# Splitting the last queries' scores of a block-causal attention into 256 and 320 columns instead of 512 and 64

## The chip, the cores and the metric

The kernel runs on one NeuronCore of a Trainium2 chip. Its engines are TensorE (PE; its weight loads are shown apart, as PEld), VectorE (DVE), ScalarE (ACT), GpSimd (POOL) and SyncE (SP, which here only issues DMAs). The metric is the device time of one execution in microseconds, lower is better. One execution was also profiled, instruction by instruction.

## What is computed

The reference is a block-causal attention, then two feed-forward layers, all in float32:

```python
# q, k, v: (4, 8, 576, 64): batch, heads, positions, head size
scores = q @ k.transpose(0, 1, 3, 2) / sqrt(64)
scores = where(pos[:, None] // 64 >= pos[None, :] // 64, scores, -1e9)
attn = exp(scores - scores.max(-1)); attn = attn / (attn.sum(-1) + 1e-9)
x = (attn @ v) as (2304, 512)
h = x @ w_in;  x = (h * sigmoid(h)) @ w_out               # w_in (512, 2048), w_out (2048, 512)
h = x @ w_in2; out = (max(h, 0) + alpha * min(h, 0)) @ w_out2
```

The last 64 of the 576 positions form the last block; their queries see all 576 keys, so no mask is needed for them.

## The kernel before

Attention goes in jobs of one batch and two heads. There are 8 `FirstJob`s and 8 jobs of kind 0 for the first 256 positions of the batches, then 16 jobs of kind 1, each for positions 256 to 575 of two heads. Beside them PE runs the first feed-forward layer: `up1` (tiles `h`) and `down1` (tiles `acc`) come in pairs of 24 products of 256 columns, all recorded at L786. The second layer follows after about 530 us with products of 384 and 512 columns, also at L786.

A product of two float32 operands is made of three matmuls (high by high, high by low, low by high part), each of which loads its own 128-column weights.

In a job of kind 1, PE has five groups beside L786. The text calls them by letters:

- B: `scores(2)`, two heads side by side, six matmuls of 384 columns at L539, into one PSUM tile `e` and the PSUM tile `s`
- C: `scores(3)`, six matmuls of 512 columns at L539, into two tiles `e`; a small product at L517 (`bound`) stands behind it
- A: `last_scores`, the 64 last queries of both heads (128 rows) against 576 keys at L539: three matmuls of 512 columns into `s`, then three of 64 columns into a tile `e`. This is what the change touches
- O: `output` at L660 (24 float16 matmuls), which in the program stands just ahead of A of the same job
- the last output at L730 (28 short matmuls), two jobs behind A

PSUM has one buffer `s` and two buffers `e`, used in turn: A of one job and B of the next share `s`. B therefore starts on `s` only when ACT has read A's scores from it.

Behind A come, on DVE, the largest score of each part (L681 and L683) and the smaller of the two negated maxima (L685); on ACT (L301) the exponentials with their sums; on DVE the sums and the reciprocal (L698, L700, L702); on POOL and DVE the weights in two float16 parts (L712, L714); then a DMA transposes them. Near A, DVE also makes the low parts `qk` of a later job's queries and keys (L504, L507), after ACT made the high parts; ACT begins that job's `qk` tile when A, the last reader of the tile's old contents, is done. L639 and L637 are weights of `scores` on DVE and POOL; L819 and L311 belong to the first layer's activation; L753 takes an output out of PSUM.

The order of everything is written by a planner at build time. Each operation is added with a cost from a formula and a due time; `Plan.order` runs through these and fixes one order for each engine. So an edit to the costs or to what waits for what can move instructions on all engines. The cost of a PE group is

```python
def pe_cost(*columns, gap=13.0):
    return sum(max(n, 56) / 2.4 + gap for n in columns) * 1e-3
```

Of the kernel before, what the change touches and what calls it, by code (L numbers as in the profile page):

```python
# [13 lines left out]
AF = mybir.ActivationFunctionType  # L14
ALU = mybir.AluOpType
AX = mybir.AxisListType
# [4 lines left out]
EPS = 1e-9  # L21
P_EXP = 14
# [187 lines left out]
def dve_cost(n, per_cycle=1, pointers=0):  # L210
    return (68 + 60 * pointers + n / 0.96 / per_cycle) * 1e-3
# [10 lines left out]
def pe_cost(*columns, gap=13.0):  # L222
    return sum(max(n, 56) / 2.4 + gap for n in columns) * 1e-3
# [3 lines left out]
def block_causal_attention_silu_prelu(  # L227
# [13 lines left out]
    nc = tc.nc  # L241
# [14 lines left out]
    add = plan.add  # L256
# [6 lines left out]
    psum = ctx.enter_context(tc.tile_pool(name="psum", bufs=1, space=PSUM))  # L263
# [31 lines left out]
    def act(n, dst, src, func, reads, writes, psum=False, **kw):  # L295
        pointers = sum(callable(kw.get(x)) for x in ("scale", "bias"))
        cost = act_cost(n, psum, pointers, "accum_out" in kw)

        def fn():
            k = {x: y() if callable(y) else y for x, y in kw.items()}  # L300
            nc.scalar.activation(dst(), src(), func, **k)  # L301

        return add("ACT", cost, fn, reads, writes)
# [162 lines left out]
    class Job:  # L466
# [203 lines left out]
        def last_scores(self):  # L670

            qk = self.qk
            x = sb(att_p, [128, 10], F32, "stat", 4, name="stat4")
            s, s2 = ps_scores(self.k), ps_scores(self.k)
            def products():
                for dst, a, b in ((s, 0, 512), (s2, 512, 576)):
                    for f in self.product(dst()[:, 0:b - a], slice(0, 128), 256, 128, a, b):
                        f()

            add("PE", pe_cost(*[512] * 3, *[100] * 3), products, [qk], [s, s2], after=self.beside(-1, "output"))  # L680
            add("DVE", dve_cost(512), lambda: nc.vector.tensor_reduce(  # L681
                x()[:, 0:1], s(), axis=AX.X, op=ALU.max, negate=True), [s], [(x, 0)])
            add("DVE", dve_cost(64), lambda: nc.vector.tensor_reduce(  # L683
                x()[:, 1:2], s2()[:, 0:64], axis=AX.X, op=ALU.max, negate=True), [s2], [(x, 0)])
            add("DVE", dve_cost(80), lambda: nc.vector.tensor_tensor(  # L685
                x()[:, 2:3], x()[:, 0:1], x()[:, 1:2], op=ALU.min), [(x, 0)], [(x, 1)])
            p = sb(att_p, [128, 512], F32, "p", 3)
            pb = sb(att_p, [128, 64], F32, "p4b", 2)
            bias = lambda: x()[:, 2:3]
            act(512, lambda: p(), lambda: s(), AF.Exp, [s, (x, 1)], [p, (x, 2)], psum=True,  # L690
                bias=bias, accum_out=lambda: x()[:, 4:5])
            act(64, lambda: pb(), lambda: s2()[:, 0:64], AF.Exp, [s2, (x, 1)], [pb, (x, 3)], psum=True,
                bias=bias, accum_out=lambda: x()[:, 5:6])
            self.xp[4] = x, p, pb

        def last_weights(self):
            x, p, pb = self.xp.pop(4)
            add("DVE", dve_cost(1, 1, 1), lambda: nc.vector.tensor_scalar(  # L698
                x()[:, 6:7], x()[:, 4:5], x()[:, 5:6], EPS, op0=ALU.add, op1=ALU.add), [(x, 2), (x, 3)], [(x, 4)])
            add("DVE", dve_cost(1), lambda: nc.vector.tensor_scalar(  # L700
                x()[:, 6:7], x()[:, 6:7], 2.0**-P_EXP, None, op0=ALU.mult), [(x, 4)], [(x, 4)])
            add("DVE", dve_cost(6), lambda: nc.vector.reciprocal(x()[:, 8:9], x()[:, 6:7]), [(x, 4)], [(x, 5)])  # L702
            rr = lambda: x()[:, 8:9]
            p16 = self.parts16(0)
            hl = lambda: p16()[:, 0:8].rearrange("p (j c) m -> p j c m", c=2)
            p3 = lambda: p().rearrange("p (j m) -> p j m", m=128)
            for src, n, hi, lo, key in (
                (p3, 512, lambda: hl()[:, :, 0], lambda: hl()[:, :, 1], 0),
                (lambda: pb(), 64, lambda: p16()[:, 8, 0:64], lambda: p16()[:, 8, 64:128], 2),
            ):  # L710
                b = pb if key else p
                add("POOL", pool_cost(n), lambda src=src, hi=hi: nc.gpsimd.tensor_scalar(  # L712
                    hi(), src(), rr(), 1.0, op0=ALU.mult, op1=ALU.mult), [b, (x, 5)], [(p16, key)])
                add("DVE", dve_cost(n, 1, 1), lambda src=src, hi=hi, lo=lo: nc.vector.scalar_tensor_tensor(  # L714
                    lo(), src(), rr(), hi(), op0=ALU.mult, op1=ALU.subtract),
                    [b, (x, 5), (p16, key)], [(p16, key + 1)])
            pT = self.pT4 = sb(att_p, [128, 9, 128], F16, "pT4")
            self.transpose(lambda: pT(), lambda: p16().rearrange("p a m -> p (a m)"), 9, [p16], [pT])

# [251 lines left out]
    for d in range(-20, total + 1):  # L971
        attend(d + 1.0)
        n, c = seq[d] if 0 <= d < total else (NB, 0)
# [37 lines left out]
    for s in range(N2 * MF + 1):  # L1011
        n, m = divmod(s, MF)
# [102 lines left out]
```

## Time and profile before

| | |
|---|---|
| Time, median of 3 runs | 977.61 us (976.92 to 980.19) |
| The profiled execution's own time | 975.61 us |
| Its span, first to last instruction | 973.8 us |
| PE busy | 956.1 us (98%) |
| DVE, ACT, POOL busy | 597.0, 398.5, 213.8 us |
| Mean granted TensorE clock | 0.998 |

The profiled execution took 1.8 us more than its span, and 2.0 us less than the median of the runs. Busy shares are averages over stages. The jobs of kind 1 lie between about 188 and 460 us; their 16 groups A start between 202 and 454 us, 16.8 us apart.

### The profile page before, as it was taken

The numbers are of one execution on the slowest core, as the hardware profiler recorded it, in microseconds if no ns is written. First come the engines' busy times: TensorE is split into PE (matmuls) and PEld (weight loads), VectorE is DVE, ScalarE is ACT, GpSimd is POOL, SyncE is SP. The second block draws the span as 40 slices with busy tenths as digits, with TensorE's granted clock in tenths as the row PEclk, the third lists the DMA queues.
The fourth block names the chain that finished last, engine by engine and source line by source line (L and its number), as shares of the span: only waits on it lengthen the run. The fifth ranks groups of instructions, "written<-read, shape, count | busy, mean of one in ns | idle before, by whom it ended". The sixth has DMA issues, their size and how long they took to land.

```text
span 973.8 us, 17935 instructions
## 1 busy us (share of the span) xinstructions
PE 956.1 (98%) x7008; PEld 882.4 (91%) x7008; DVE 597.0 (61%) x1343; ACT 398.5 (41%) x928; POOL 213.8 (22%) x262
## 2 busy tenths in 40 slices
PE   7799999999999999999999999999999999999998
PEld 4699999999999999999999999999999999999997
DVE  4899966578877778776113899544443444434443
ACT  7997645455555555553234656211211211211111
POOL 0002313344545445453234200100100100100000
PEclk9999999999999999999999999999999999999999
DMA  9941243356565656564116950010100200000100
GB/s 366 346 198 49 59 115 87 101 111 120 136 143 127 125 129 138 109 133 79 33 55 225 368 209 1 1 66 1 33 33 0 65 1 1 33 1 1 33 1 33
DMA packets 124468, 94.04 MB, mean 97 GB/s; under 512 B 98400, under 2 KB 109792, under 8 KB 124384
## 3 DMA queue, kind: packets, MB, share of 16 engines
q1 hardware_dynamic: 124384, 92.90, 34.4%
q8 instruction: 55, 0.90, 0.4%
q14 instruction: 29, 0.24, 0.1%
HBM read 60.37 MB, written 9.96 MB: 72 GB/s over the span
## 4 chain that ended last, share of the span: by engine, by line
PE 89%; DMA 5%; DVE 3%; ACT 1%; issue 1%; POOL 0%; SPq 0%; POOLq 0%; DVEq 0%; ACTq 0%
PE h L786 29%; PE acc L786 27%; PE e L786 16%; PE s L786 7%; DMA raw0i<-w_in 4%; PE e L539 3%; PE o L660 2%; PE s L539 2%; PE o L730 1%; PE o L517 1%; DMA pT<-p 1%; DVE p L639 1%; DMA raw1i<-w_in 0%; ACT p L301 0%; POOL p L637 0%
## 5 line engine op out<-in xcount | busy, mean ns | idle before, releaser
L786 PE MATMUL h<-xh,w0i 128*128 128x256 f32 x1728 | 229.2, 287 | 1.0 <-DVE w0i L344 0.6
L786 PEld LDWEIGHTS h<-xh,w0i 128*128 128x128 f32 x1728 | 215.8, 193 | 3.5 <-DVE w0i L344 1.0
L786 PE MATMUL acc<-g,w0o 128*128 128x256 f32 x1536 | 201.2, 285 | 0.1
L786 PEld LDWEIGHTS acc<-g,w0o 128*128 128x128 f32 x1536 | 189.7, 192 | 1.6 <-issue 0.5
L301 ACT ACTIVATE g<-u 128x384 fp32r<-128x384 f32 x96 | 50.2, 523 | 270.0 <-DVE u L904 270.0
L786 PE MATMUL e<-w1o,g 128*128 128x512 f32 x576 | 148.8, 394 | 0.0
L786 PEld LDWEIGHTS e<-w1o,g 128*128 128x128 f32 x576 | 106.8, 188 | 16.7
L786 PE MATMUL h<-xh,w1i 128*128 128x384 f32 x576 | 109.1, 337 | 0.0
L786 PE MATMUL acc<-xh,w1i 128*128 128x384 f32 x576 | 108.8, 337 | 0.0
L786 PEld LDWEIGHTS h<-xh,w1i 128*128 128x128 f32 x576 | 102.3, 188 | 4.1
L786 PEld LDWEIGHTS acc<-xh,w1i 128*128 128x128 f32 x576 | 102.4, 188 | 4.0
L311 POOL TENSOR_TENSOR g<-t,g 128x512 fp32r<-128x512 f32 x56 | 77.7, 1387 | 86.6 <-ACT g L301 84.4
L819 DVE SCALAR_TENSOR_TENSOR t<-t,h 128x512 f32<-128x512 f32 x72 | 49.1, 682 | 65.0 <-ACT t L301 64.8
L311 DVE TENSOR_TENSOR g<-u,g 128x384 fp32r<-128x384 f32 x96 | 54.5, 567 | 54.7 <-ACT g L301 54.7
L637 POOL TENSOR_SCALAR p<-p,stat 128x384 f16<-128x384 f32 (+3 forms) x96 | 61.9, 651 | 99.4 <-DVE stat L626 36.4
L786 PE MATMUL s<-w1o,g 128*128 128x512 f32 x288 | 82.0, 393 | 0.0
L311 POOL TENSOR_TENSOR xh<-xs,xh 128x384 fp32r<-128x384 f32 x24 | 25.0, 1071 | 255.0 <-ACT xh L301 255.0
L301 ACT ACTIVATE t<-h 128x512 f32<-128x512 f32 x72 | 43.2, 599 | 82.2 <-PE h L786 77.5
L639 DVE SCALAR_TENSOR_TENSOR p<-p,stat,p 128x384 f16<-128x384 f32 (+3 forms) x96 | 68.6, 730 | 10.4 <-POOL p L637 10.1
L902 DVE TENSOR_SCALAR u<-acc,alpha_sb 128x384 f32<-128x384 f32 x48 | 29.6, 618 | 73.4 <-PE acc L786 73.4
L902 DVE TENSOR_SCALAR u<-h,alpha_sb 128x384 f32<-128x384 f32 x48 | 29.7, 618 | 69.7 <-PE h L786 69.5
L786 PEld LDWEIGHTS s<-w1o,g 128*128 128x128 f32 x288 | 54.1, 188 | 12.5
(113 smaller groups left out, 1154.7 us busy)
## 6 DMA issues: line engine op xcount, KB each, us to landing
st<-qkv_b SPq DMA_DIRECT2D x16, 800.0 KB, 4.7
raw0i<-w_in SPq DMA_DIRECT2D x16, 512.0 KB, 10.2
raw0o<-w_out SPq DMA_DIRECT2D x16, 512.0 KB, 10.2
raw1i<-w_in SPq DMA_DIRECT2D x16, 512.0 KB, 5.7
raw1o<-w_out SPq DMA_DIRECT2D x16, 512.0 KB, 5.6
x<-x2e SPq DMA_DIRECT2D x18, 256.0 KB, 3.4
st<-qkv_first SPq DMA_DIRECT2D x8, 512.0 KB, 8.2
st<-qkv_a SPq DMA_DIRECT2D x8, 512.0 KB, 3.9
```

The lines of the kernel that those rows point to most:

```text
L301: nc.scalar.activation(dst(), src(), func, **k)
L311: eng.tensor_tensor(lo(), src(), hi().bitcast(F32), op=ALU.subtract)
L517: add("PE", 0.25, lambda: nc.tensor.matmul(t()[:, 0:128], am()[:, 0:1].to_broadcast([128, 128]), eye_sb(), start=True, stop=True), [am, ey ...
L539: yield lambda n=n, a=a, b=b: nc.tensor.matmul(dst, w[rows, a, q0:q0 + m], w[rows, b, nq + k0:nq + k1], start=(n == 0), stop=(n == 2))
L637: add("POOL", pool_cost(n), lambda hl=hl, rr=rr, pr=pr: nc.gpsimd.tensor_scalar(hl()[:, :, 0], pr(), rr(), 1.0, op0=ALU.mult, op1=ALU.mult ...
L639: add("DVE", dve_cost(n, 1, 1), lambda hl=hl, rr=rr, pr=pr: nc.vector.scalar_tensor_tensor(hl()[:, :, 1], pr(), rr(), hl()[:, :, 0], op0=A ...
L660: nc.tensor.matmul(o()[64 * r:64 * r + 64, q0:T1], self.v(r, kt, cv), self.pT[r][1]()[:, 2 * kt + cp, q0:T1], start=(kt == 0 and n == 0), ...
L730: nc.tensor.matmul(o()[64 * r:64 * r + 64, 0:64], self.v(r, kt, cv), pT()[:, run, 64 * r:64 * r + 64], start=(run == 0 and cv == 0), stop= ...
L786: nc.tensor.matmul(dst, lhs(a), rhs(b), start=(start and n == 0), stop=(stop and n == 2))
L819: add("DVE", dve_cost(2 * T1), lambda: nc.vector.scalar_tensor_tensor(t(), t(), 1.0, h3(), op0=ALU.add, op1=ALU.mult), [t, h], [t])
L902: add("DVE", dve_cost(T2, 1, 1), lambda: nc.vector.tensor_scalar(u(), h()[:, 0:T2], 0.0, alpha_sb()[:, m:m + 1], op0=ALU.min, op1=ALU.mult ...
```

## The change

The 576 keys are divided at 256 instead of at 512. A becomes three matmuls of 256 columns into `s` and three of 320 columns into `e`. The two reductions take 256 and 320 columns. The exponentials become three instead of two: 256 columns from `s`, 256 columns and 64 columns from `e`, so that the tiles `p` and `pb` hold the same as before. The three sums are added in one instruction; the small constant and the scale go into the next one.

```diff
             def products():
-                for dst, a, b in ((s, 0, 512), (s2, 512, 576)):
+                for dst, a, b in ((s, 0, 256), (s2, 256, 576)):
...
-            add("PE", pe_cost(*[512] * 3, *[100] * 3), products, [qk], [s, s2], after=self.beside(-1, "output"))
-            add("DVE", dve_cost(512), lambda: nc.vector.tensor_reduce(
-                x()[:, 0:1], s(), axis=AX.X, op=ALU.max, negate=True), [s], [(x, 0)])
-            add("DVE", dve_cost(64), lambda: nc.vector.tensor_reduce(
-                x()[:, 1:2], s2()[:, 0:64], axis=AX.X, op=ALU.max, negate=True), [s2], [(x, 0)])
+            add("PE", pe_cost(*[256] * 3, *[320] * 3), products, [qk], [s, s2], after=self.beside(-1, "output"))
+            add("DVE", dve_cost(256), lambda: nc.vector.tensor_reduce(
+                x()[:, 0:1], s()[:, 0:256], axis=AX.X, op=ALU.max, negate=True), [s], [(x, 0)])
+            add("DVE", dve_cost(320), lambda: nc.vector.tensor_reduce(
+                x()[:, 1:2], s2()[:, 0:320], axis=AX.X, op=ALU.max, negate=True), [s2], [(x, 0)])
...
-            act(512, lambda: p(), lambda: s(), AF.Exp, [s, (x, 1)], [p, (x, 2)], psum=True,
-                bias=bias, accum_out=lambda: x()[:, 4:5])
-            act(64, lambda: pb(), lambda: s2()[:, 0:64], AF.Exp, [s2, (x, 1)], [pb, (x, 3)], psum=True,
-                bias=bias, accum_out=lambda: x()[:, 5:6])
+            for dst, src, n, c in (
+                (lambda: p()[:, 0:256], lambda: s()[:, 0:256], 256, 4),
+                (lambda: p()[:, 256:512], lambda: s2()[:, 0:256], 256, 5),
+                (lambda: pb(), lambda: s2()[:, 256:320], 64, 6),
+            ):
+                part = (pb, (x, c)) if c == 6 else ((p, c), (x, c))
+                act(n, dst, src, AF.Exp, [s if c == 4 else s2, (x, 1)], part, psum=True,
+                    bias=bias, accum_out=lambda c=c: x()[:, c:c + 1])
...
-                x()[:, 6:7], x()[:, 4:5], x()[:, 5:6], EPS, op0=ALU.add, op1=ALU.add), [(x, 2), (x, 3)], [(x, 4)])
+                x()[:, 7:8], x()[:, 4:5], x()[:, 5:6], x()[:, 6:7], op0=ALU.add, op1=ALU.add),
+                [(x, 4), (x, 5), (x, 6)], [(x, 7)])
...
-                x()[:, 6:7], x()[:, 6:7], 2.0**-P_EXP, None, op0=ALU.mult), [(x, 4)], [(x, 4)])
-            add("DVE", dve_cost(6), lambda: nc.vector.reciprocal(x()[:, 8:9], x()[:, 6:7]), [(x, 4)], [(x, 5)])
+                x()[:, 7:8], x()[:, 7:8], EPS, 2.0**-P_EXP, op0=ALU.add, op1=ALU.mult), [(x, 7)], [(x, 7)])
+            add("DVE", dve_cost(6), lambda: nc.vector.reciprocal(x()[:, 8:9], x()[:, 7:8]), [(x, 7)], [(x, 8)])
```

The new lines move the later ones: L786 of before is L791 of the change, L730 is L735, L819 is L824, L753 is L758, and L698, L700 and L702 are L702, L705 and L707.

The planner answers with another order from the first group A on. PE, from A of the eighth job of kind 1 to B of the next job, before:

```order
L539 MATMUL s<-qk 128x512 x3
L539 MATMUL e<-qk 128x64 x3
L786 MATMUL acc<-g,w0o_914 128x256 x12
L786 MATMUL acc<-g,w0o_945 128x256 x12
L786 MATMUL h<-xh_3078,w0i_1154 128x256 x12
L539 MATMUL e<-qk 128x384
L539 MATMUL s<-qk 128x384
```

The same place on PE in the changed kernel:

```order
L539 MATMUL s<-qk 128x256 x3
L539 MATMUL e<-qk 128x320 x3
L791 MATMUL acc<-g,w0o_914 128x256 x12
L791 MATMUL acc<-g,w0o_945 128x256 x12
L539 MATMUL e<-qk 128x384
L539 MATMUL s<-qk 128x384
```

B moved ahead of 12 products of `up1`: it stands 24 instead of 36 products behind A. So it is in 10 of the 15 jobs that have a B behind their A; in the other five it is 42, 36, 30, 27 and 27 products. Before, it stood 36 products behind in 11 of the 15 jobs. C moved with it: in most jobs from 30 products ahead of the next O to 48, in three to 36.

DVE at the same place, from the activation L819 of the first layer to the sums behind A, before:

```order
L819 SCALAR_TENSOR_TENSOR t<-t,h 128x512
L639 SCALAR_TENSOR_TENSOR p_4713<-p,stat,p_4713 128x4x128
L639 SCALAR_TENSOR_TENSOR p_4716<-p,stat,p_4716 128x4x128
L753 SCALAR_TENSOR_TENSOR xh_4180<-o,sc,xh_4180 128x256
L681 TENSOR_REDUCE stat_4746<-s 128x1
L504 SCALAR_TENSOR_TENSOR qk<-st,qk 128x384
L683 TENSOR_REDUCE stat_4746<-e 128x1
L507 TENSOR_TENSOR qk<-st,qk 128x576
L685 TENSOR_TENSOR stat_4746<-stat_4746 128x1
```

The same place on DVE in the changed kernel:

```order
L639 SCALAR_TENSOR_TENSOR p_4690<-p,stat,p_4690 128x4x128
L824 SCALAR_TENSOR_TENSOR t<-t,h 128x512
L639 SCALAR_TENSOR_TENSOR p_4720<-p,stat,p_4720 128x4x128
L758 SCALAR_TENSOR_TENSOR xh_4187<-o,sc,xh_4187 128x256
L681 TENSOR_REDUCE stat_4747<-s 128x1
L683 TENSOR_REDUCE stat_4747<-e 128x1
L685 TENSOR_TENSOR stat_4747<-stat_4747 128x1
L504 SCALAR_TENSOR_TENSOR qk<-st,qk 128x384
L507 TENSOR_TENSOR qk<-st,qk 128x576
```

One of the two weights of C (L639) moved ahead of the activation, and the two reductions and their minimum moved ahead of both low parts of `qk`. ACT keeps its order up to here: the three instructions of the later job's `qk`, then the exponentials of A.

## Rows read from the trace of the kernel before

**Rows 1.** The page: busy us (share of span) and instructions.
```profile
PE 956.1 (98%) x7008; PEld 882.4 (91%) x7008; DVE 597.0 (61%) x1343; ACT 398.5 (41%) x928; POOL 213.8 (22%) x262
```

**Rows 2.** Windows: busy us (instructions) of PE, PEld, DVE, ACT, POOL; then clock, DMA.
```profile
200.00:460.00 260.00, 259.83 (x2579) 239.32 (x2578) 205.16 (x520) 134.69 (x338) 123.54 (x154) 1.00 0.60 125
```

**Rows 3.** Waits by engine, 200 to 460 us: us in total, times, longest.
```profile
PEld s L539 <- ACT p L301: 0.6, 2, 0.4
```

**Rows 4.** Chain that ended last, 316 to 328 us: start us, us, engine, tile, line.
```profile
319.99 0.89 PE s L539 x3
320.88 0.25 PE e L539 x3
321.13 2.95 PE acc L786 x24
324.08 1.44 PE h L786 x12
325.52 0.37 PE e L539
```

**Rows 5.** The same view, longest pieces: 24 products with no other group around.
```profile
461.76 2.88 PE acc L786 x24
```

**Rows 6.** The same view, 153 to 160 us: 256-column scores of a kind 0 job.
```profile
154.99 0.61 PE o L660 x12
155.60 0.55 PE s L539 x3
156.16 1.42 PE h L786 x12
```

**Rows 7.** The same view, 700 to 712 us: 512 and 384 columns, layer 2.
```profile
701.53 0.69 PE s L786 x3
702.22 2.10 PE acc L786 x12
```

**Rows 8.** Timeline of ACT, 317.5 to 326 us: start us, us [idle before].
```profile
321.17 0.74 ACT L301 ACTIVATE qk<-st 128x640 fp32r<-128x640 f32 x1
...
322.03 1.10 ACT L301 ACTIVATE qk<-st 128x384 fp32r<-128x384 f32 x2
324.11 0.69 ACT L301 ACTIVATE p<-s,stat 128x512 f32<-128x512 f32 x1 [0.98 <-DVE stat L685]
324.70 0.19 ACT L301 ACTIVATION_READ_ACCUMULATOR p<-s,stat 128x1 f32 x1
```

**Rows 9.** Timeline of DVE, 317.5 to 327 us.
```profile
319.38 0.69 DVE L819 SCALAR_TENSOR_TENSOR t<-t,h 128x512 f32<-128x512 f32 x1 [0.90 <-ACT t L301]
319.99 1.41 DVE L639 SCALAR_TENSOR_TENSOR p<-p,stat,p 128x512 f16<-128x512 f32 x2
321.31 0.48 DVE L753 SCALAR_TENSOR_TENSOR xh<-o,sc,xh 128x256 fp32r<-128x256 f32 x1
...
323.20 0.75 DVE L507 TENSOR_TENSOR qk<-st,qk 128x576 fp32r<-128x576 f32 x1
323.87 0.15 DVE L685 TENSOR_TENSOR stat<-stat 128x1 f32<-128x1 f32 x1
```

**Rows 10.** Timeline of PE, 317.5 to 327 us: B's first matmul.
```profile
325.45 0.44 PE L539 MATMUL e<-qk 64*128 64x384 f32 x1
```

**Rows 11.** Chain, 236 to 258 us: a job in which B waits.
```profile
239.08 0.60 DVE stat L681
...
241.69 0.20 ACT p L301
...
241.94 0.44 PE s L539
```

**Rows 12.** Groups by form, whole span: line, engine, shapes, count, busy us, mean ns.
```profile
L301 ACT ACTIVATE p<-s,stat 128x256 f32<-128x256 f32 x16 | 7.9, 495 | 1.2 <-DVE stat L591 1.2
...
L591 DVE TENSOR_REDUCE stat<-s 128x2 f32<-128x256 f32 x6 | 2.4, 407 | 0.0
```

More of the change, by code (lines that the diff above doesn't have):

```diff
@@ L712, in last_weights @@
                 add("POOL", pool_cost(n), lambda src=src, hi=hi: nc.gpsimd.tensor_scalar(
-                    hi(), src(), rr(), 1.0, op0=ALU.mult, op1=ALU.mult), [b, (x, 5)], [(p16, key)])
+                    hi(), src(), rr(), 1.0, op0=ALU.mult, op1=ALU.mult), [b, (x, 8)], [(p16, key)])
                 add("DVE", dve_cost(n, 1, 1), lambda src=src, hi=hi, lo=lo: nc.vector.scalar_tensor_tensor(
                     lo(), src(), rr(), hi(), op0=ALU.mult, op1=ALU.subtract),
-                    [b, (x, 5), (p16, key)], [(p16, key + 1)])
+                    [b, (x, 8), (p16, key)], [(p16, key + 1)])
             pT = self.pT4 = sb(att_p, [128, 9, 128], F16, "pT4")
```

## The prediction, made before the changed kernel ran

> **What bounds the kernel.** I read the page first: PE is busy for 956.1 of 973.8 us [rows 1], so nothing but PE can be worth much. An average can hide a stage with another limit, so the windows come next: from 200 to 460 us, where the 16 groups A stand, PE is busy in 259.83 of 260.00 us at a granted clock of 1.00, which is the 2.4 GHz level, while ACT works for 134.69, POOL for 123.54 and DVE for 205.16 us [rows 2]. In that stretch PE's weight loads waited for ACT for 0.6 us in all, twice [rows 3]. So in this stage a change is worth what it takes off PE's own time, less the waits that it makes.
>
> Busy time does not say what a matmul costs in a stream, since matmuls overlap. The chain of waits does: it gives each piece from the end of the one before to its own end, and the chain runs through PE in these jobs [rows 4].
>
> **What group A costs now.** Behind O, the three matmuls of 512 columns take 0.89 us and the three of 64 columns 0.25 us. The 24 products behind them take 2.95 us [rows 4], where 24 undisturbed ones take 2.88 us [rows 5]: 0.07 us more. Together 0.89 + 0.25 + 0.07 = 1.21 us. If columns alone counted, three matmuls of 64 would cost 64/512 of three of 512, and three undisturbed ones of 512 take 0.69 us [rows 7]: 0.09 us. They cost 0.25 + 0.07 = 0.32 us, that is 0.107 us each. Each matmul loads 128 columns of weights, and behind 64 columns such a load finds too little work to hide under; the 0.07 us are the next product's load, which hides badly under the last short matmul.
>
> The Trainium skill bears on this twice, on one page, "TensorE: Matmul & The Clock Gate". Its section "Back-to-back issue gap" puts a warm matmul at N/2.4 + 2.5 ns. By that, as an estimate, 512 and 64 columns take 215.8 + 29.2 ns and 256 and 320 take 109.2 + 135.8 ns, both 245 ns, and the change would bring nothing. Its section "LDWEIGHTS (loading the stationary operand)" puts a load at P/1.2 ns, an estimate of 107 ns for 128 columns. By that rule a short matmul costs as much as its load; the trace agrees, with the 0.107 us above.
>
> **What it will cost.** 256 columns: the chain has the very case, in a job of kind 0, behind an O as here: 0.55 us for three, and the 12 products behind them take 1.42 us, half of 2.88 within 0.02 us, so nothing is left over [rows 6]. 320 columns stand nowhere in the trace. Bounds: 12 matmuls of 384 take 2.10 us, 0.175 us each [rows 7], and 12 of 256 take 0.12 us each, from 2.88/24 [rows 5]. 320 is halfway, and between 256, 384 and 512 (0.23 each) the price rises evenly by about 0.055 us for 128 columns, so I take 0.147 us, 0.44 us for three. The new A is 0.55 + 0.44 = 0.99 us, 0.22 us less than 1.21. For 16 jobs that is **3.5 us**. With 320 at the price of 256 it would be (1.21 - 0.55 - 0.36) x 16 = 4.8 us, at that of 384 (1.21 - 0.55 - 0.525) x 16 = 2.2 us.
>
> **What is added elsewhere.** DVE: two reductions of 256 and 320 columns for two of 512 and 64. One of 256 takes 0.407 us [rows 12], the old one of 512 took 0.60 us in the chain [rows 11]; in sum the columns are the same and DVE is not the bound. ACT: two exponentials of 256 columns at 0.495 us [rows 12] for one of 512 at 0.69 us [rows 8], so about 0.3 us more for each job, 5 us in all. It lies beside PE: ACT is idle for 125 of the 260 us [rows 2], and what follows these exponentials (the sums, the weights, the transposing DMA) feeds the last output at L730, which stands two jobs, some 33 us, behind. The sums keep three small DVE instructions. I cost all this at nothing. Uncovered, the ACT part would be those 5 us.
>
> **What is moved.** B stands 24 products behind A in ten jobs, 1.44 us sooner than with 36. What it waits for is the tile `s`, until ACT's exponential has read A's scores; behind B on PE stand L730 and all of `up1`, so a late `s` delays PE in full. I follow the eighth job, with A's new times.
>
> - PE: O ends at 319.99 [rows 4], A at 319.99 + 0.99 = 320.98, 24 products at 323.86. B's first matmul started 0.07 us before the end of the chain piece ahead of it (325.45 [rows 10] against 325.52 [rows 4]), so it will want to start at 323.79.
> - ACT: the `qk` instructions started 0.04 us behind the end of A (321.13 and 321.17) and lasted to 322.03 + 1.10 = 323.13, 1.96 us [rows 4, 8]. From 321.02 they last to 322.98. The exponential of `s` then takes 0.495 us, to 323.48. Where B did wait, it started on `s` 0.25 us behind the start of the sum's read (241.94 and 241.69) [rows 11]; that read starts 0.1 us before the exponential ends (324.70 and 324.80) [rows 8]. So `s` is free at about 323.63.
> - DVE: the exponential also needs L685. Behind L819 (to 320.07) come one L639 (half of 1.41 us), L753 (0.48) [rows 9], L681 (0.41), L683 (between 0.41 and 0.60, say 0.48) and L685 (0.15): 322.29, or 0.7 us before ACT is ready. Before, two L639 and both low parts of `qk` stood ahead, and L685 ended at 324.02 [rows 9].
>
> So `s` is free 0.16 us before B asks for it, and no wait is added; the margin is thin. The two old waits, in jobs with 36 and 30 products now, lose products and gain a shorter exponential; I leave their 0.6 us as they are. C moves by at least 0.7 us away from the O that reads its weights, so those DMAs get more time; SP issues the same ones.
>
> **Sum.** 975.61 - 3.5 = 972.1 us for the profiled execution. The median of the runs is 2.0 us above that one, so 977.6 - 3.5 = **974.1 us** is the forecast, 0.36% less. About 0.3%, 2.9 us, is what a measurement of this kernel can tell from no change, so even a correct sum lies near the edge.
>
> **The rivals.**
>
> 1. *B waits a little.* The margin of 0.16 us comes out of 2.5 us of ACT work added from single rows. If ACT is 0.2 to 0.4 us slower, B waits 0.04 to 0.24 us in ten jobs: 0.4 to 2.4 us back, 974.5 to 976.5 us. From 0.06 us of wait on, the gain is under 0.3%. For it: ACT has three exponentials in a row, and two of them must end before the next stages. Against it: `s` needs only the first. Chance 0.24, and of that most counts as "same".
> 2. *Only columns count, and the division changes nothing.* Then 977.6 us. The rows on the 64-column matmuls speak against it; for it, only that 320 columns were never seen. Chance 0.08. The Trainium skill's page on TensorE gives this result too, by its "Back-to-back issue gap".
> 3. *The wait for `s` becomes the new bound, slower.* If L685 ends as late as before (324.02), the exponential of 256 columns runs from 324.11 [rows 8] to 324.61, `s` is free at 324.76, and B is 0.97 us late in ten jobs and 0.61 us in the two with 27 products: +10.9 - 3.5 = +7.4 us, 985.0 us. It decides from 0.64 us of wait in ten jobs ((3.5 + 2.9)/10). Against it: the new order puts L685 ahead of both low parts. For it: L639 has to run first and waits for POOL. Chance 0.06.
>
> **How the numbers follow.** The forecast (no added wait) has 0.62. Its own range, from the bounds for 320 columns, is 972.8 to 975.4 us. The range reaches up to no change, 977.6 us, and down to 4.8 us plus the 0.6 us of old waits, 972.2, less half a microsecond of scatter: 971.7. Out of it stay rival 3 and scatter. Faster: 0.6 (the forecast, without the runs in which scatter hides it). Same: 0.34. Slower: 0.06.
>
> **What would show it.** In the chain, A at 0.55 and 0.44 us and 24 products of 2.88 us wherever B does not cut in. In the waits of PE's weight loads, L539 behind ACT at no more than 0.6 us. Wrong would be: 320 columns at 0.175 us or more, a residue behind them, or a wait of B on `s` in the ten jobs.

## The result, and the profile after

The change made the kernel slower: 986.14 us (985.43 to 987.48, 6 runs) against 977.3 us (975.52 to 980.19, 6 runs) of the kernel before on the same chip, a ratio of 1.009 [1.0073, 1.0107]; in brackets, here and below, the 95% interval. That is under 1%, but clear of the scatter. The forecast was 974.1 us and its range ended at 977.6. One of the ten runs of e3 below took 2347 us in a slow state, and e3's median of 977.08 leaves it out, where expectations that say 977.4 include it.

The profiled execution's span is 984.4 us, 10.5 more than before. Of that, 1.8 us stand ahead of the first group A, where every engine still runs the same instructions in the same order (A ends at 205.06 instead of 203.24 us), so they are no effect of the change. In the jobs, from the first to the fifteenth A, PE needed 14 x 17.35 us where it had needed 14 x 16.81, which is 7.6 us; the last 1.1 us stand behind the fifteenth A.

The page and the window of the jobs, in the columns of [rows 1, 2]. PE, which was busy for 259.83 of 260 us, is now idle for 6 us there, and DVE is busy for 17 us more:

```profile
PE 958.9 (97%) x7008; PEld 883.8 (90%) x7008; DVE 618.4 (63%) x1343; ACT 402.2 (41%) x960; POOL 210.1 (21%) x262
200.00:460.00 260.00, 254.05 (x2483) 232.68 (x2482) 222.00 (x512) 135.30 (x358) 117.68 (x151) 1.00 0.58 123
```

The waits in the same stretch, as in [rows 3]. The 0.6 us in two waits have become 9.7 us in 15, one behind each A that a B follows. The prediction had named such a wait as a sign that it is wrong:

```profile
PEld s L539 <- ACT p L301: 9.7, 15, 1.2
PE s L539 <- ACT p L301: 5.8, 12, 0.9
```

The prediction's eighth job on PE, the place of [rows 10]. B starts on its tile `e` at 329.05 and on `s` at 329.88, 0.83 us later:

```profile
329.05 0.44 PE L539 MATMUL e<-qk 64*128 64x384 f32 x1
329.88 0.44 PE L539 MATMUL s<-qk 64*128 64x384 f32 x1 [0.39 <-ACT p L301]
```

Before, `s` started together with `e` (its row is in [rows 10]):

```profile
325.45 0.44 PE L539 MATMUL s<-qk 64*128 64x384 f32 x1
```

Only 0.39 us of the 0.83 are idle. For the rest, `e`'s first matmul ran alone, where before it had run beside that of `s`: PE counts as busy, and the time is lost all the same. So the idle time of PE shows about half of what a late `s` costs. From the traces, the starts of `s` behind those of `e`, added up over the 15 jobs, come to 12.4 us, and to 1.1 us in the kernel before.

The chain that ended last tells more than the waits do. In [rows 4] it ran through PE alone. Here it is after the change, from 327 to 345 us (start us, us, engine, tile, line):

```profile
327.43 0.82 ACT qk L301 x2
328.28 0.69 ACT qk L301 x2
...
329.28 1.00 ACT p L301 x4
330.28 0.30 ACT p4b L301 x2
330.61 0.28 DVE stat L702
...
331.27 0.11 DVE e L596
...
331.90 0.55 DVE stat L598
...
332.51 1.25 POOL v L548
...
335.12 0.60 POOL p L637
335.78 0.82 issue
336.60 1.65 DVE p L639
338.25 0.19 DVE e L596 x2
...
341.41 0.70 POOL p L637
...
343.23 0.69 DVE t L824
343.96 0.51 issue
344.47 0.72 ACT qk L301
```

No matmul stands in it. It goes from ACT (the later job's `qk`, A's three exponentials) to DVE (the sum of the three at L702, B's maxima at L598), to POOL (L548, the `v` of a later job) and DVE (weights), to C's maxima, to C's weights on POOL, back to the activation L824 and to ACT's `qk`, 17.04 us later. So ACT, DVE and POOL, none of them busy for more than 86% of the window, form a loop that takes longer than PE's work of a job, and PE waits once in each round. Utilization doesn't show this; the chain does.

### The profile page after: what moved, and what is told of

Same layout as the page of the kernel before. It is cut to its first block, busy times and chain, and to the rows that moved or that the text cites. A ratio compares the mean times of both kernels' runs of the same rounds, so it can differ in the third digit from the quotient of the medians.

```text
span 984.4 us, 18006 instructions
## 1 busy us (share of the span) xinstructions
PE 958.9 (97%) x7008; PEld 883.8 (90%) x7008; DVE 618.4 (63%) x1343; ACT 402.2 (41%) x960; POOL 210.1 (21%) x262
## 4 chain that ended last, share of the span: by engine, by line
PE 64%; DVE 13%; ACT 8%; issue 7%; DMA 4%; POOL 4%; POOLq 0%; ACTq 0%; SPq 0%; DVEq 0%
PE h L791 21%; PE acc L791 18%; PE e L791 16%; PE s L791 7%; ACT p L301 4%; DVE p L639 3%; DVE stat L598 2%; POOL p L637 2%; DMA pT<-p 1%; ACT qk L301 1%; DVE t L824 1%; POOL v L548 1%; DMA raw0i<-w_in 1%; DVE p L719 1%; PE s L539 1%
## 5 line engine op out<-in xcount | busy, mean ns | idle before, releaser
L791 PE MATMUL h<-xh,w0i 128*128 128x256 f32 x1728 | 228.4, 287 | 0.6 <-DVE w0i L344 0.3
L791 PEld LDWEIGHTS h<-xh,w0i 128*128 128x128 f32 x1728 | 215.9, 193 | 3.2 <-issue 0.8
L791 PE MATMUL acc<-g,w0o 128*128 128x256 f32 x1536 | 198.6, 284 | 0.1
L791 PEld LDWEIGHTS acc<-g,w0o 128*128 128x128 f32 x1536 | 189.7, 192 | 1.3 <-issue 0.5
L791 PE MATMUL e<-w1o,g 128*128 128x512 f32 x576 | 148.8, 393 | 0.0
L791 PEld LDWEIGHTS e<-w1o,g 128*128 128x128 f32 x576 | 106.7, 188 | 16.8
L791 PE MATMUL h<-xh,w1i 128*128 128x384 f32 x576 | 109.1, 337 | 0.0
L791 PE MATMUL acc<-xh,w1i 128*128 128x384 f32 x576 | 108.7, 337 | 0.0
L791 PEld LDWEIGHTS h<-xh,w1i 128*128 128x128 f32 x576 | 102.3, 188 | 4.2
L791 PEld LDWEIGHTS acc<-xh,w1i 128*128 128x128 f32 x576 | 102.4, 188 | 4.1
L639 DVE SCALAR_TENSOR_TENSOR p<-p,stat,p 128x384 f16<-128x384 f32 (+3 forms) x96 | 83.7, 888 | 25.7 <-POOL p L637 25.0
L311 POOL TENSOR_TENSOR g<-t,g 128x512 fp32r<-128x512 f32 x56 | 76.4, 1364 | 101.9 <-ACT g L301 101.0
L311 DVE TENSOR_TENSOR g<-u,g 128x384 fp32r<-128x384 f32 x96 | 54.5, 567 | 54.4 <-ACT g L301 54.4
L824 DVE SCALAR_TENSOR_TENSOR t<-t,h 128x512 f32<-128x512 f32 x72 | 49.0, 680 | 55.9 <-ACT t L301 55.8
L791 PE MATMUL s<-w1o,g 128*128 128x512 f32 x288 | 81.9, 392 | 0.0
L311 POOL TENSOR_TENSOR xh<-xs,xh 128x384 fp32r<-128x384 f32 x24 | 25.0, 1070 | 255.0 <-ACT xh L301 255.0
L637 POOL TENSOR_SCALAR p<-p,stat 128x384 f16<-128x384 f32 (+3 forms) x96 | 58.1, 615 | 92.7 <-DVE stat L626 41.2
L301 ACT ACTIVATE p<-e,stat 128x384 f32<-128x384 f32 (+3 forms) x94 | 52.7, 565 | 46.2 <-DVE stat L598 42.5
```

The lines of the kernel that those rows point to most:

```text
L311: eng.tensor_tensor(lo(), src(), hi().bitcast(F32), op=ALU.subtract)
L637: add("POOL", pool_cost(n), lambda hl=hl, rr=rr, pr=pr: nc.gpsimd.tensor_scalar(hl()[:, :, 0], pr(), rr(), 1.0, op0=ALU.mult, op1=ALU.mult ...
L639: add("DVE", dve_cost(n, 1, 1), lambda hl=hl, rr=rr, pr=pr: nc.vector.scalar_tensor_tensor(hl()[:, :, 1], pr(), rr(), hl()[:, :, 0], op0=A ...
L791: nc.tensor.matmul(dst, lhs(a), rhs(b), start=(start and n == 0), stop=(stop and n == 2))
L824: add("DVE", dve_cost(2 * T1), lambda: nc.vector.scalar_tensor_tensor(t(), t(), 1.0, h3(), op0=ALU.add, op1=ALU.mult), [t, h], [t])
```

## The experiments

All times are medians beside runs of the kernel before on the same chip (975.7 to 976.9 us). The ratio to these is estimated over the runs and can differ from that of two medians by up to 0.15%. "The order" is that of the instructions on every engine; "the division" is 256/320 or 512/64. The code shows the deciding lines of an edit; "..." marks what is left out.

### Is it the order or the work?

**e1** does the change's work in the order of before. The planner gets the costs of before, and the first two exponentials are one operation for it.

```diff
-            add("PE", pe_cost(*[256] * 3, *[320] * 3), products, [qk], [s, s2], after=self.beside(-1, "output"))
+            add("PE", pe_cost(*[512] * 3, *[100] * 3), products, [qk], [s, s2], after=self.beside(-1, "output"))
...
+            add("ACT", act_cost(512, True, 1, True), exps, [s, s2, (x, 1)], [p, (x, 4), (x, 5)])
```

> The division into 256 and 320 columns alone: the matmuls, reductions and exponentials of the change, but every cost and dependency that the planner sees is that of before, so each engine keeps the order of before. Theory 1 (the new order costs the time, the division itself gains): 16 x 0.23 us less, 973.6 us, ratio 0.996; PE's weight loads wait for ACT at L539 for at most 1 us. Theory 2 (the division itself costs it, because ACT has a third exponential and is late for B in any order): 982 to 987 us, with waits of some 9 us at L539.

**e2** does the work of before in the change's order (the planner gets the change's costs and an empty third operation).

> The new order alone: 512 and 64 columns, two reductions and two exponentials as before, but planned as the change is, so each engine has the order of the change. Theory 1 (the order costs the time): slower than the change by the 3.7 us of group A and by up to 0.2 us in 15 jobs, because the tile s is read by an exponential of 512 columns: 989 to 993 us, ratio 1.012 to 1.016. Theory 2 (the division costs it): about 977 us.

Measured: e1 990.61 us, ratio 1.0157 [1.0142, 1.0172]; e2 978.2 us, 1.0021 [1.001, 1.0032]. My first theory, that the new order costs the time, fell: the order alone costs 0.2%, and the work in the old order costs more than in the new one.

**e3** keeps the change and puts B's weights L639 a little later in the plan, so that C's maxima come ahead of them on DVE, in the trace one ahead of each. The planner then moves other instructions too: B stands 24 to 30 products behind A.

```diff
+                plan.at += 0.05 if i == 2 else 0.0
                 add("DVE", dve_cost(n, 1, 1), lambda hl=hl, rr=rr, pr=pr: nc.vector.scalar_tensor_tensor(
...
+                plan.at -= 0.05 if i == 2 else 0.0
```

> The change, with the two low parts of B's weights (L639) due 0.05 later in the plan on DVE, so that they come behind the largest scores of C. Theory 1a (these two, which take 2.5 us beside the activation on POOL where they were planned at 1.1, delay C's largest scores, then its weights, the activation L824, ACT's qk and with it the tile s): the waits of L539 for ACT fall from 9.7 us to under 3 us, 975 to 980 us. Theory 1b (24 products between A and B are too few, whatever DVE does first): waits stay near 9 us, 983 to 987 us.

**e4** plans L639 with 0.85 us in place of the formula's cost, nearer to what it takes (in the jobs of kind 1 alone).

> The change, with L639 of the jobs of kind 0 and 1 planned at 0.85 us, its mean in the trace, instead of 0.53 and 0.66. The plan then puts B 33 to 42 products behind A. Theory 1 (the planner took DVE for faster than it is and so moved B and C to places where their inputs are late): 973 to 977 us, waits at L539 under 2 us. Theory 1b (24 products are too few whatever DVE does): the same, because B stands later. Theory 2 (the division itself): 982 to 987 us.

Measured: e3 977.08 us, 1.0012 [1.0002, 1.0022]; e4 985.3 us, 1.0101 [1.0086, 1.0116]. An order can hide almost all of the loss (e3), but a truer cost for one instruction didn't lead the planner to it (e4). What is left in e3 mostly shows in no wait; in the eighth job `s` starts 0.29 us behind `e`:

```profile
323.97 0.44 PE L539 MATMUL e<-qk 64*128 64x384 f32 x1
324.26 0.44 PE L539 MATMUL s<-qk 64*128 64x384 f32 x1
```

### Which part of the work?

**e6** leaves the division as before and makes only the exponential of 512 columns in two halves. **e5** has the division without the third exponential: it leaves the last 64 columns out, and POOL and DVE take 64 other columns in their place, so that their work stays the same. **e7** has all the change's work and gives PE back its old length. All three stand in the order of before.

```diff
 # e6, against e1
-                for dst, a, b in ((s, 0, 256), (s2, 256, 576)):
+                for dst, a, b in ((s, 0, 512), (s2, 512, 576)):
...
 # e5, against e1
-            act(64, lambda: pb(), lambda: s2()[:, 256:320], AF.Exp, [s2, (x, 1)], [pb, (x, 6)], psum=True,
-                bias=bias, accum_out=lambda: x()[:, 6:7])
...
 # e7, against e1
+                for _ in range(2):
+                    nc.tensor.matmul(s()[:, 0:256], w[0:128, 0, 256:384], w[0:128, 0, nq:nq + 256], start=True, stop=True)
```

> The division of the kernel before (512 and 64 columns) and its order, but the exponential over 512 columns is made as two over 256, so that ScalarE has three for A as in the change. Theory 'third instruction': 985 to 991 us, with waits of B on the tile s in most jobs. Rival 'TensorE earlier': 977 to 979 us, at most two such waits, as in the kernel before.

> The 256/320 division in the order of the kernel before, without A's third exponential (the one over 64 columns and its sum are left out; POOL and DVE take 64 other columns in its place, so that they do the same amount of work). The order of every engine is otherwise that of the run that gave 990.6 us. Theory 'third instruction': ScalarE's extra exponential, about 0.27 us more from the exponential of s to the last one, is what keeps the chain on VectorE, ScalarE and GpSimd longer than TensorE's work of a job: 973 to 978 us, B's waits for the tile s mostly under 0.7 us. Rival 'TensorE earlier': it is that A ends 0.23 us sooner and so meets the same chain earlier: 988 to 991 us, B's waits above 1 us as they were.

> The 256/320 division in the order of the kernel before, with two more matmuls of 256 columns into s ahead of A's own (their result is overwritten), so that A takes TensorE 0.99 + 0.24 = 1.23 us, about the 1.21 us of before. Theory 'third instruction': stays at 989 to 992 us, since ScalarE's work is that of the run that gave 990.6. Rival 'TensorE earlier': back to 977 to 979 us.

Measured: e6 990.62 us, 1.0149 [1.0134, 1.0164]; e5 983.73 us, 1.008 [1.0064, 1.0095]; e7 991.11 us, 1.0157 [1.014, 1.0174]. Beside three exponentials PE's length has no part in it: e7 is as slow as e1. The third exponential by itself costs as much as all of the change's work did in this order: e6, whose matmuls are those of before, waits for `s` in 14 jobs. Its waits on PE's side:

```profile
PEld s L539 <- ACT p L692: 11.6, 14, 1.2
PE s L539 <- ACT p L692: 8.0, 14, 0.9
```

The added ACT work is small. In the eighth job e6's exponentials last from 331.65 us to the end of the last sum's read at 332.98, 1.33 us; before, they lasted from 324.11 [rows 8] to 325.19, 1.08 us. The sum behind them, with three terms, takes 0.27 instead of 0.21 us. Those 0.31 us a job are 5 us in 16 jobs, near the prediction's "about 0.3 us more"; they cost 15. And e5, whose two exponentials last 1.02 us, is still 8 us slow. Its two reductions hold DVE no longer than before (0.73 against 0.72 us in the fourth job, from their starts to the next one's), but PE's job is 0.23 us shorter in it. Something makes much of small shifts.

### What multiplies them?

DVE's L639 and POOL's L311 lengthen each other. Timeline of DVE and POOL in the fourth job, kernel before:

```profile
252.89 1.75 DVE L639 SCALAR_TENSOR_TENSOR p<-p,stat,p 128x512 f16<-128x512 f32 x2
254.01 1.79 POOL L311 TENSOR_TENSOR g<-t,g 128x512 fp32r<-128x512 f32 x1 [0.57 <-DVE p L639]
```

The same two rows of e5:

```profile
252.98 2.88 DVE L639 SCALAR_TENSOR_TENSOR p<-p,stat,p 128x512 f16<-128x512 f32 x2
254.01 1.29 POOL L311 TENSOR_TENSOR g<-t,g 128x512 fp32r<-128x512 f32 x1 [0.40 <-ACT g L301]
```

The DVE row begins 0.09 us later, and the pair takes 2.88 instead of 1.75 us. In the kernel before, the second L639 started at 253.91, 0.10 us ahead of L311, and it was L311 that became long. In e5 it started at 254.08, 0.07 us behind. The Trainium skill has a rule for this, on the page "SBUF — State Buffer", section "Who interferes with whom": a DVE instruction with two inputs in SBUF and a GpSimd instruction that reads SBUF share a port pair as an exclusive lock, so whichever is issued first keeps it and the other waits. These rows agree. L311 hangs on O, and so on PE; L639 hangs on the maxima and exponentials. So DVE's chain, once 0.1 to 0.2 us late against L311, loses 1.1 us more. It went like this throughout: in jobs 4 to 15 of the kernel before, the second L639 started 0.10 to 0.45 us ahead of L311; in e5 it started 0.04 to 0.06 us behind it in nine of these twelve jobs, at the same moment in one, and took 1.78 to 1.85 us in these ten.

**e8** takes L311's work in the units beside the jobs from POOL to DVE, in the change's order.

```diff
-            eng = nc.gpsimd if lo_engine == "POOL" else nc.vector
+            eng = nc.gpsimd if (run_on or lo_engine) == "POOL" else nc.vector
...
-              "DVE" if n < FIRST else "POOL")
+              "DVE" if n < FIRST else "POOL", "DVE")
```

> The change as it is, but the low parts of g in the feed-forward units (L311, 128x512) are taken by VectorE instead of GpSimd, at the same place of the order: VectorE has about 0.69 us more for each (48 of them), GpSimd 1.36 us less. Theory 'L639 is slow beside GpSimd's L311' (0.60 us alone, 1.34 us beside it): L639 falls to about 0.6 to 0.7 us, B's waits on s go under 0.5 us, 972 to 977 us. Rival 'VectorE is simply too full': it gets 48 x 0.69 = 33 us more work, of which the jobs have about 3 each: 990 us or more, with the waits on VectorE longer.

Measured: 980.46 us, 1.0046 [1.0031, 1.0061], between the two forecasts. The contention has its share: L311 on DVE rose from 11.1 to 50.7 us (56 more of them, not 48), and yet the kernel lost 4.8 us against the kernel before on its chip where the change lost 8.8. In the traces the jobs, from the first to the fifteenth A, took 17.12 us each instead of 17.35. L639 of 384 columns fell from a mean of 1195 ns after the change to 751 (groups by form, DVE):

```profile
L639 DVE SCALAR_TENSOR_TENSOR p<-p,stat,p 128x512 f16<-128x512 f32 x32 | 30.0, 950 | 13.2 <-POOL p L637 13.1
L639 DVE SCALAR_TENSOR_TENSOR p<-p,stat,p 128x384 f16<-128x384 f32 x32 | 23.1, 751 | 1.0 <-POOL p L637 0.4
```

The 950 ns of the 512 columns are two prices: 16 of the 32 run beside POOL's L637 and take 1.16 us, the other 16 take 0.74.

**e9, e10, e11, e15** asked whether the late state keeps itself alive, so that one kick decides. e9 (on e1), e11 (on the change) and e15 (on e5) delay PE once; e10 delays DVE once in the kernel before.

```diff
 # e9, e11, e15: ahead of O's own matmuls, in one job
...
+                    for _ in range(13 if len(outputs) == 2 else 0):
+                        for r in range(2):
+                            nc.tensor.matmul(o()[64 * r:64 * r + 64, 0:T1], self.v(r, 0, 0), self.pT[r][1]()[:, 0, 0:T1],
+                                             start=True, stop=True)
 # e10: C's reciprocal in one job
...
+                for _ in range(4 if thirds.count(3) == 4 and i == 3 else 1):
+                    nc.vector.reciprocal(x()[:, 8:10], x()[:, 6:8])
```

> The 256/320 division in the order of the kernel before (990.6 us so far), with one addition: ahead of O in a single one of the 16 jobs, the one whose A is at about 236 us, TensorE makes 26 more matmuls of 256 columns into o (overwritten by O's own), some 1.5 us of work in all. Theory 'two phases': in each job C's second L639 on VectorE and GpSimd's L311 start within 1 us of each other, and whichever starts first has its way; when L311 is first, L639 takes 1.8 us in place of 0.74, VectorE stays late, B waits, and the next job is the same. L311 hangs on O, L639 on the maxima, so one delay of O lets L639 start first, and from there the jobs follow TensorE: 974 to 979 us, faster by more than 10 us for 1.5 us of work more, with no waits of B on s after 260 us. Rival 'the chain with three exponentials is longer than TensorE's job by itself': the waits come back within a job or two, 989 to 992 us.

> The kernel before, with one addition: in a single one of the 16 jobs the reciprocal of C's sums (L626, two elements a partition, ahead of its L637) is made four times instead of once, about 0.5 us of VectorE's time in the whole program, at about 251 us, where L639 got ahead of L311 by 0.1 us. Theory 'two phases': L639 comes behind L311 again, VectorE stays late for some jobs or for all of the rest, 0.4 to 0.6 us of TensorE each: 979 to 985 us. Rival 'a delay is taken up once': 976 to 978 us, no more than 0.5 us over the kernel before.

> The change as it is (986.1 us), with the same 26 matmuls more ahead of O in a single job, the one whose A is at about 238 us. Theory 'two phases': in the change's own order L311 meets B's pair of L639 instead (2.50 us where the same order with the old division has 1.35), and the one delay frees it too: 974 to 980 us. Rival 'in this order the chain is longer than TensorE's job by itself': 985 to 988 us.

> The division in the old order without the third exponential (983.7 us), plus 26 matmuls more ahead of O in one job, at about 236 us, some 1.5 us. In the kernel before, a job in which L639 came first took 16.42 us from L639 to L639 by its own chain, and one in which it came second about 17.3; TensorE's job with the division is 16.54. Theory 'a race that is lost by under 0.1 us': the one delay lets L639 win, and without the third exponential it stays ahead: 974 to 978 us. Rival 'the division in this order has a chain over 16.54 in any case': the waits come back and the time is 984 to 986 us.

Measured: e9 993.7 us, 1.0177 [1.0159, 1.0194]; e10 978.4 us, 1.0016 [1.0006, 1.0025]; e11 987.1 us, 1.0097 [1.0074, 1.012]; e15 983.93 us, 1.007 [1.0054, 1.0086]. As a theory of two states that each last, this fell. e9 was free for one job and e11 too; then the waits came back. e10, between its two forecasts, fell back and freed itself several times over, for 1.5 us in all. e15 stayed free for three jobs. Timeline of PE, the 320-column matmuls of A in five jobs of e15 that follow each other:

```profile
239.32 0.61 PE L541 MATMUL e<-qk 128*128 128x320 f32 x3
255.87 0.60 PE L541 MATMUL e<-qk 128*128 128x320 f32 x3
272.40 0.60 PE L541 MATMUL e<-qk 128*128 128x320 f32 x3
288.94 0.60 PE L541 MATMUL e<-qk 128*128 128x320 f32 x3
305.99 0.60 PE L541 MATMUL e<-qk 128*128 128x320 f32 x3
```

The first three steps are 16.54 us, which is PE's job with the new division; the fourth is 17.05, and from there they stay at 17.3. In the three free jobs the second L639 started 0.42, 0.34 and 0.12 us ahead of L311, in the next one 0.05 us behind it. So in this order the loop of the other engines has hardly any room under 16.54 us even when L639 comes first. Under the 16.77 us of before it had enough to recover, in the kernel before and in e10. That PE's shorter job by itself is what e5 loses by is argued from this; no run gives e5 PE's old length.

### Without the third exponential, in other orders

**e14** is the change in its own order without the third exponential (the 64 columns left out as in e5). **e16** is e3 without it. **e17** is e3's order with the division and the exponentials of before.

```diff
 # e14 and e16
+                if c == 6:
+                    add("ACT", act_cost(n, True, 1, True), lambda: None, [s2, (x, 1)], part)
+                    continue
...
```

> The change as it is, without A's third exponential (left out with its sum; GpSimd and VectorE take 64 other columns in its place; every engine's order otherwise that of the change). Theory 'the third exponential is 0.45 us in a chain that is already as long as TensorE's job': B's waits of about 0.83 us fall to 0.4 or less: 976 to 981 us. Rival 'the order of the change costs it': 984 to 987 us.

> The change with C's maxima ahead of B's weights on VectorE (977.4 us) and without A's third exponential (left out with its sum; GpSimd and VectorE take 64 other columns in its place). Theory 'the saving on TensorE shows as soon as the chain is shorter than its job': B's waits of 0.28 us go with the 0.45 us of the exponential, A to A is 16.54 us, and the time is 972 to 975 us. Rival 'the saving isn't to be had': 976 to 978 us.

> The kernel before's division and exponentials (512 and 64 columns) in that same order with C's maxima first. By the theory A to A is TensorE's 16.77 us from the first job on, without the waits of the first three jobs: 975.5 to 977 us, and 2 to 4 us over the run with the 256/320 division and no third exponential. By the rival the two take the same.

Measured: e14 977.79 us, 1.0007 [0.9992, 1.0022]; e16 975.21 us, 0.9989 [0.9981, 0.9998]; e17 981.37 us, 1.0053 [1.0041, 1.0065]. e14 settles the change's own order: of its 8.8 us, between 7 and 8 hang on the third exponential. With that gone, the chain is mostly on PE again (81% of it on the page, 64% after the change, 89% before). But e14 isn't the forecast's 974.1 either: `s` starts behind `e` by 6.3 us in all. A piece of the chain in e14, with A at the price that was forecast:

```profile
320.83 0.55 PE s L539 x3
321.38 0.44 PE e L539 x3
321.81 2.87 PE acc L795 x24
```

All the medians side by side, in us, with the difference from the kernel before on the same chip:

| order of | 512/64, two exponentials | 512/64, three | 256/320, two (64 columns left out) | 256/320, three |
|---|---|---|---|---|
| before | 975.7 to 977.3 | 990.6, +14.9 (e6) | 983.7, +8.1 (e5) | 990.6, +13.9 (e1) |
| the change | 978.2, +1.5 (e2) | not run | 977.8, +1.4 (e14) | 986.1, +8.8 |
| C's maxima first | 981.4, +5.2 (e17) | not run | 975.2, -1.0 (e16) | 977.1, +0.4 (e3) |

Beside the 256/320 division the third exponential costs about 6, 7 and 1 us in the three orders, and 15 us beside 512/64 in the order of before. The division without it costs +8, 0 and -6 us. Neither has one price for the whole; each is worth what the loop makes of it in the order at hand.

How much the loop takes can be read at B. The starts of `s` behind those of `e`, added up over the 15 jobs of a trace, were 14.5 us in e6, 12.1 in e5, 17.5 in e1, 3.2 in e2, 6.3 in e14, 12.4 in the change, 5.3 in e17, 4.1 in e16 and 5.0 in e3. What each of these has over the 1.1 us of before, less the forecast's 3.5 us where A is divided at 256, gives its difference in the table to within 1.6 us. So PE's gain fits every row, and what was lost was lost where B waited for `s`.

### Moves that should have shortened the loop

**e12** (on the change) and **e13** (on e3) move ACT's copies into `qk` behind A's exponentials, and DVE's L504 and L507 behind B's maxima (in their traces L505 and L508). **e18** (on e3) moves only the copy of 576 keys, behind A's first exponential.

```diff
 # e18 moves j.late[1::2] and stops at ahead.exp
+                for late, mark in ((j.late[:2], ahead.exp), (j.late[2:], nxt.maxima)):
+                    late = [o for o in ops[:ops.index(mark)] if o in late]
...
+                    at = ops.index(mark) + 1
+                    ops[at:at] = late
```

> The change (986.1 us) with two places moved and the work unchanged: the copies of q and k into qk (L301, 384 and 576 columns, 1.1 us on ScalarE) stand behind A's three exponentials instead of ahead of them, and L504 and L507 (1.3 us on VectorE) behind B's maxima. Theory 'length of the chain': A's exponentials and all that follows them in the chain come up to 0.7 us earlier in each job, which takes most of B's 0.83 us: 975 to 980 us. Rival 'TensorE has to wait elsewhere': the copies are in the chain wherever they stand: 984 to 987 us.

> The same two moves in the kernel with C's maxima first (977.4 us), where B waited some 0.28 us a job and A to A took 16.82 us. Theory 'length of the chain': B's waits go, A to A is TensorE's 16.54 us, and the time is 977.4 - 16 x 0.28 = 973 us, under both kernels. Rival: 977 us, unchanged.

> The order with C's maxima first (977.4 us, all three exponentials, all the work), with one instruction moved on ScalarE alone: the copy of 576 keys into qk (0.67 us) stands behind A's first exponential instead of ahead of it. Theory: A's first exponential ends up to 0.3 us earlier (L685 ends at 2.13 us behind A, the exponential started at 2.49), B's waits of 0.28 us go, A to A falls from 16.82 towards 16.54 us: 973 to 975 us, under the kernel before. Rival 'the chain through the third exponential and L702 is as long as the job anyway': 976.5 to 978 us.

Measured: e12 995.7 us, 1.0185 [1.0166, 1.0204]; e13 986.43 us, 1.0096 [1.0078, 1.0114]; e18 981.27 us, 1.0046 [1.0032, 1.0059]. All three missed by much: each starts A's first exponential sooner behind the smaller of the two negated maxima and makes the rest of the round longer. Timeline of DVE in the eighth job of e13, where the sum of A's parts is L710:

```profile
328.82 0.27 DVE L710 TENSOR_SCALAR stat<-stat 128x1 f32<-128x1 f32 x1 [1.45 <-ACT p4b L301]
...
330.56 0.56 DVE L505 SCALAR_TENSOR_TENSOR qk<-st,qk 128x384 fp32r<-128x384 f32 x1
331.05 0.75 DVE L508 TENSOR_TENSOR qk<-st,qk 128x576 fp32r<-128x576 f32 x1
```

And of e18, where it is L708:

```profile
326.30 0.76 DVE L508 TENSOR_TENSOR qk<-st,qk 128x576 fp32r<-128x576 f32 x1 [0.79 <-ACT qk L301]
327.06 0.27 DVE L708 TENSOR_SCALAR stat<-stat 128x1 f32<-128x1 f32 x1
```

The low parts of `qk` had run while DVE waited for A's last exponential. Moved behind B's maxima (e13, and e12 alike), they left that wait empty, 1.45 us where e3 has 0.45, and put about 1.2 us between B's maxima and the next weights. In e18 A's first exponential started 0.09 us behind the smaller maximum, 0.35 in e3. But the moved copy now ran between the exponentials: L508 waited for it until 326.30, the sum of A's last exponential was read out only at 327.02, and DVE's sum began 2.02 us behind that maximum, where it was 1.68 in e3. What counted in these runs is the length of the whole round, and not how soon ACT reads `s`. No kernel that does all the work beat the one before; e3 comes within 0.12% of it.

## Why the prediction was wrong

- **Group A's price: right.** 0.55 and 0.44 us and no residue, as the piece of e14 shows. The 0.22 us a job are real: PE's job without a wait fell from 16.77 to 16.54 us.
- **"I cost all this at nothing": the step that failed.** The size was right (0.25 us measured, about 0.3 foreseen) and the cover was wrong: without the third exponential the change ran in 977.8 us (e14), with it in 986.1. The prediction followed the exponentials to the last output, two jobs behind, and stopped. It didn't ask what else is queued on DVE behind the sum that waits for the last exponential. There stand B's memsets and maxima, and through them B's exponentials, weights and all the rest of the loop. The change's own row, at the same job, shows the wait that leads there:

```profile
330.61 0.27 DVE L702 TENSOR_SCALAR stat<-stat 128x1 f32<-128x1 f32 x1 [0.45 <-ACT p4b L301]
```

- **"What is moved": wrong in its inputs.** The prediction took the start times of before for DVE and ACT and changed only A. It priced L639 at half of 1.41 us and let ACT's `qk` start 0.04 us behind A. Measured: the second L639 ended at 327.52, 1.26 us behind A's end (326.26), where the forecast had it 0.21 ahead of it; `qk` began 1.17 us behind A, because `g` waited 1.11 us for L824 and L824 stood behind the first L639. `s` came 0.83 us late, where 0.16 us of margin were forecast. This step has a share of its own: the new order without the third exponential (e14) still lost the 3.5 us and about 1 more.
- **Idle time was taken for room.** "ACT is idle for 125 of the 260 us" is true and says nothing about room, since what ACT waits for here is a link of a loop through three engines. The loop's length was never worked out. In the kernel before, the jobs with a wait took 17.17 and 17.35 us, which already showed a loop longer than PE's 16.77.
- **The rivals.** Rival 3 had the place, the sign and nearly the size (985.0 against 986.1 us) and was given 0.06. It expected L685 2.89 us behind A as before; it came 2.66 behind, and the exponential then waited for ACT. It also named L639 and its wait for POOL. That the size came so near is partly luck: it had 0.97 us in ten jobs and 0.61 in two, and `s` came 0.35 to 1.39 us behind `e` in all fifteen. Rival 1, a wait of 0.04 to 0.24 us, was too small. Rival 2 is out by A's price: three matmuls of 64 columns cost 0.32 us before, where its formula gives 0.09. That formula stands in the Trainium skill (page "TensorE: Matmul & The Clock Gate", section "Back-to-back issue gap") for a matmul by itself; for a stream of loads and matmuls the section says that both set the spacing, and these rows agree.

What stays open: how long the loop is by itself in each order, and why in the old order it has room under 16.77 us but not under 16.54. That turns on starts 0.04 to 0.1 us apart, and no run set those apart one by one.

## What to carry to other kernels

Before calling work on an idle engine free, list what is queued behind each instruction that waits for its result, on every engine, and follow that until it returns to where it began; if the round is about as long as the bound engine's job, the work is not free and can cost more than its length (here about 0.3 us a job cost from 0.1 to 0.9). A cut on the bound engine is worth no more than the room that this round leaves. And an instruction more (two halves for one) has a price of its own, so a division that saves on one engine is to be priced with the number of instructions that it makes on the next.

## What the hardware showed that was not expected

Two DVE instructions of one shape differed by nearly three times. Timeline of DVE in a job of e3 (L639 of the change is L640 there):

```profile
313.96 1.70 DVE L640 SCALAR_TENSOR_TENSOR p<-p,stat,p 128x384 f16<-128x384 f32 x1
315.59 0.68 DVE L598 TENSOR_REDUCE stat<-e 128x1 f32<-128x512 f32 x1
316.19 0.60 DVE L640 SCALAR_TENSOR_TENSOR p<-p,stat,p 128x384 f16<-128x384 f32 x1
...
321.89 0.47 DVE L685 TENSOR_REDUCE stat<-e 128x1 f32<-128x320 f32 x1
322.40 0.91 DVE L687 TENSOR_TENSOR stat<-stat 128x1 f32<-128x1 f32 x1
```

POOL at the same time:

```profile
313.95 1.30 POOL L311 TENSOR_TENSOR g<-t,g 128x512 fp32r<-128x512 f32 x1
...
321.99 1.30 POOL L311 TENSOR_TENSOR g<-t,g 128x512 fp32r<-128x512 f32 x1 [2.55 <-ACT g L301]
```

The first L640 started 0.01 us behind L311 and took 1.70 us; the second, alone, 0.60. L687, one element a partition with two inputs, took 0.91 us beside L311; as L685 of the kernel before it took 0.15 [rows 9]. The reduction beside it (L685 here), with one input, kept its time: 0.47 us, and 0.48 in e5 where POOL was idle. So a mean by line hides two prices, and in the rows shown a start 0.01 to 0.1 us earlier decides which one holds.
